# Gated attention and feed-forward on one core: value products in blocks of four key tiles from the first head, and three query products put off

## The chip, the core and the metric

One core of a Trainium2 chip runs the whole kernel. The metric is the device time of one execution in microseconds (us). The core's engines are TensorE (PE: matmuls, with weight loads as PEld), VectorE (DVE), ScalarE (ACT), GpSimdE (POOL) and SyncE (SP, which issues nearly all DMAs here). Each engine has its own instruction queue and works it off in order; engines wait for each other through semaphores. PE writes to PSUM, a small memory that ACT or DVE must empty before PE can use the same buffer again.

## What is computed

Input x has 2048 rows (tokens) of 512. There are 32 query heads of width 16, but one key and one value head; beside it a gated feed-forward of width 1792; a sigmoid gate per token mixes both.

```python
q = (x @ wq).reshape(B, S, 32, 16)          # 32 heads
k, v = x @ wk, x @ wv                       # one head
p = softmax(q @ k.T * 16 ** -0.5)           # per head, 2048 x 2048
a = (p @ v over all heads) @ wo
b = (silu(x @ w_gate) * (x @ w_up)) @ w_down
g = sigmoid((x * gate_w).sum(-1))
out = g * a + (1 - g) * b
```

All is float32. Projections are made of three products of rounded halves (high by high, high by low, low by high), so every operand is kept as a pair of tiles, `h` and `l`.

## The kernel before

**Numbering.** Token columns come in four chunks c of 512 (`CH`), query weights in four groups m of 128 columns (eight heads each), keys in 16 key tiles of 128. Query product (m, c) is the 128 x 512 piece of the queries for group m and chunk c; there are 16.

**Opening.** x is transposed chunk by chunk on PE, keys and values are projected, and the four query products of group 0 are made one after the other. Each is taken out of PSUM by `keep` (L208): a rounded copy `qh`, the rest `ql` by a subtraction, and a bound `qb` (|q| times the largest key, L218 or L221 and L222), whose maximum goes to `top` (L238). For group 0, `qh` and `qb` are made by ACT (L217, L218), for the others all by DVE. The pieces lie in tiles `hh` and `hl`, with seven buffers each; a buffer is free again when the DMA that stores it to `q_d` in DRAM (L232) has landed. SP issues the twelve stores of group 0 together (`run(STORES, NCH)`, L630), then the load of the last query weights (`load_wq(3)`, L631). Then `fill(GAP)` makes three more query products in full, (1,0), (1,1), (1,2). Heads after head 0 read their rows back from `q_d` (`load_head`, L640).

**Attention and feed-forward side by side.** From L771 on the order of instructions is written by hand. `score(u, j)` makes one half of a score tile (128 keys by 1024 queries, two matmuls on the two row halves of the array) into one of two PSUM buffers `pss`. `exps` takes the exponential on ACT into a tile `pt`. `mix(u)` makes the value products of tile u (L680) into `po`: they use the array in four column strips, unlike everything around them. In between, `feed` puts steps of a job list: each step is up to two matmuls on half the array's rows, the low rows of one job and the high rows of an earlier one (`Halves.step`, L385). Jobs are the query products, then the feed-forward's gate, up and down products. They use three PSUM buffers `pf`; when the high rows of a job are done, its end function empties the buffer.

**The order.** For heads 0 and 1 (32 tiles) a loop of `BEGIN = 16` rounds (L774 to L795) makes two tiles a round: four score halves, eight steps, then the value products of two tiles; all exponentials are taken by ACT straight from PSUM (form "A"). Then one longer block (`TURN`, L801) makes ten score halves, all of form "A", so that scores run two tiles ahead. From there on `block` (L711) makes four tiles a time by the string `STEPS`: eight score halves, 16 steps, then the value products of four tiles. In it three of the eight halves are of form "H": DVE copies the upper 512 columns out of PSUM (L664), ACT takes the exponential of the lower 512 from PSUM and of the upper 512 later from SBUF. Six `pt` buffers are needed for blocks; three come from pool `bp`, three from pool `bp2`, which is opened only when the last query product is made, in the memory of the query weights and of the x chunks 2 and 3 (`open_acc`, L248).

**Rows of x.** Chunks 0 and 1 stay in `xpool`; chunks 2 and 3 lie in `qpool` until the queries are done, are stored to `x_d`, and are read back (`load_x_again`) when the feed-forward has finished chunk 0 and chunk 1.

**End.** After the last block nine jobs are left; they run in full, and then the output projection (`finish`) closes the program.

## Time and profile before

| | |
|---|---|
| median of 3 runs (lowest, highest) | 1345.32 us (1343.87, 1346.47) |
| the profiled execution's own time | 1344.01 us |
| span of its instructions | 1341.9 us |
| mean granted TensorE clock | 0.999 |
| DVE, ACT, POOL busy, share of the span | 54%, 79%, 29% |
| DMA | 107.79 MB, 80 GB/s in the mean |

The span is 2.1 us shorter than the profiled execution's time; that is what lies around it. Rows of the timeline give start and duration in us, engine, line, operation, the tile written and the tiles read, and how many instructions the row merges; in brackets stands how long the engine was idle before, and what ended that. "SPq" is SP issuing a DMA.

### The profile page before, as it was taken

The numbers are of one execution on the slowest core, as the hardware profiler recorded it, in microseconds if no ns is written. First come the engines' busy times: TensorE is split into PE (matmuls) and PEld (weight loads), VectorE is DVE, ScalarE is ACT, GpSimd is POOL, SyncE is SP. The second block draws the span as 40 slices with busy tenths as digits, with TensorE's granted clock in tenths as the row PEclk, the third lists the DMA queues.
The fourth block names the chain that finished last, engine by engine and source line by source line (L and its number), as shares of the span: only waits on it lengthen the run. The fifth ranks groups of instructions, "written<-read, shape, count | busy, mean of one in ns | idle before, by whom it ended". The sixth has DMA issues, their size and how long they took to land. (4 is left out here: it accounts for less than half of the span.)

```text
span 1341.9 us, 26802 instructions
## 1 busy us (share of the span) xinstructions
PE 1328.0 (99%) x10743; PEld 770.4 (57%) x10743; DVE 722.4 (54%) x1221; ACT 1061.6 (79%) x1463; POOL 391.0 (29%) x408
## 2 busy tenths in 40 slices
PE   9999999999999999999999999999999999999997
PEld 7655555555555555555555555555555555555576
DVE  5554565555455555555464555455454565465432
ACT  4578888888888888888888888888888888888400
POOL 6140321152042151152131241142131241333343
PEclk9999999999999999999999999999999999999999
DMA  8455221131122221141131221231121221222154
GB/s 277 142 173 190 65 60 38 35 107 44 44 86 77 78 80 38 35 107 44 52 122 39 82 79 39 57 83 45 52 61 30 81 79 39 74 68 60 44 161 143
DMA packets 101489, 107.79 MB, mean 80 GB/s; under 512 B 9968, under 2 KB 69616, under 8 KB 99696
## 3 DMA queue, kind: packets, MB, share of 16 engines
q1 hardware_dynamic: 99632, 105.81, 27.5%
q8 instruction: 88, 1.44, 0.5%
q10 hardware_dynamic: 1728, 0.20, 0.1%
q14 instruction: 41, 0.34, 0.1%
HBM read 76.09 MB, written 29.36 MB: 79 GB/s over the span
## 5 line engine op out<-in xcount | busy, mean ns | idle before, releaser
L668 ACT ACTIVATE pt<-pss 128x1024 f32<-128x1024 f32 (+1 forms) x1024 | 842.0, 876 | 177.3 <-PE pss L660 146.3
L664 DVE COPY pt<-pss 128x512 f32<-128x512 f32 x354 | 244.8, 692 | 415.6 <-PE pss L660 380.6
L680 PE MATMUL po<-pt,vaug 128*32 128x512 f32 x4096 | 467.6, 595 | 0.0
L660 PE MATMUL pss<-qs,ks 64*128 64x512 f32 x2048 | 403.1, 417 | 1.1 <-ACT pt L668 1.1
L660 PEld LDWEIGHTS pss<-qs,ks 64*128 64x128 f32 x2048 | 193.7, 184 | 218.4 <-ACT pt L668 183.6
L680 PEld LDWEIGHTS po<-pt,vaug 128*32 128x32 f32 x4096 | 119.2, 109 | 260.2 <-issue 255.2
L668 ACT ACTIVATE pt<-pt 128x512 f32<-128x512 f32 x354 | 195.7, 620 | 0.0
L176 PE MATMUL pf<-xh,wgl 64*128 64x512 f32 (+1 forms) x440 | 162.0, 392 | 0.0
L176 PE MATMUL pf<-xh,wgh 64*128 64x512 f32 (+1 forms) x440 | 160.5, 391 | 0.5 <-DVE acc L331 0.2
L176 PE MATMUL pf<-xl,wgh 64*128 64x512 f32 (+1 forms) x440 | 160.2, 390 | 0.0
L176 PE MATMUL pf<-xh,wuh 64*128 64x512 f32 (+1 forms) x440 | 158.4, 391 | 0.7 <-DVE sign L403 0.3
L176 PE MATMUL pf<-xl,wuh 64*128 64x512 f32 (+1 forms) x440 | 158.2, 390 | 0.0
L176 PE MATMUL pf<-xh,wul 64*128 64x512 f32 (+1 forms) x440 | 157.3, 391 | 0.0
L106 POOL CAST wgh<-wraw 128x512 fp32r<-128x512 f32 x56 | 36.1, 644 | 402.6 <-PE pf L176 311.8
L176 PE MATMUL pf<-wdh,hh 64*128 64x512 f32 (+1 forms) x427 | 143.4, 391 | 1.7 <-DVE hh L106 1.7
L176 PE MATMUL pf<-wdh,hl 64*128 64x512 f32 (+1 forms) x427 | 144.1, 390 | 0.0
L176 PE MATMUL pf<-wdl,hh 64*128 64x512 f32 (+1 forms) x427 | 143.4, 390 | 0.0
L689 DVE RECIPROCAL rsb<-rsb 128x128 f32<-128x128 f32 x128 | 117.1, 935 | 10.1 <-issue 8.2
L106 POOL CAST wuh<-wraw 128x512 fp32r<-128x512 f32 x56 | 35.1, 626 | 298.2 <-PE pf L176 245.3
L176 PEld LDWEIGHTS pf<-xh,wgh 64*128 64x128 f32 (+1 forms) x440 | 78.5, 185 | 9.8 <-issue 2.5
L176 PEld LDWEIGHTS pf<-xh,wuh 64*128 64x128 f32 (+1 forms) x440 | 77.3, 185 | 9.3 <-issue 3.7
L176 PEld LDWEIGHTS pf<-xl,wgh 64*128 64x128 f32 (+1 forms) x440 | 78.5, 185 | 6.0
(157 smaller groups left out, 1547.6 us busy)
## 6 DMA issues: line engine op xcount, KB each, us to landing
wraw<-in_B_w_gate_dram SPq DMA_DIRECT2D x56, 256.0 KB
wraw<-in_B_w_up_dram SPq DMA_DIRECT2D x56, 256.0 KB
wraw<-in_B_w_down_dram SPq DMA_DIRECT2D x56, 256.0 KB
qs<-q_d SPq DMA_DIRECT2D x62, 192.0 KB
q_d<-hl SPq DMA_DIRECT2D x18, 256.0 KB
q_d<-hh SPq DMA_DIRECT2D x18, 256.0 KB
o_d<-osb SPq DMA_DIRECT2D x128, 32.0 KB
a_d<-acc SPq DMA_DIRECT2D x4, 1024.0 KB
```

The source lines that it names most:

```text
L106: eng_hi.tensor_copy(hi, src)
L176: ins = nc.tensor.matmul(self.ps, a, b, start=(i == 0 and not half), stop=(last and half != 0))
L660: nc.tensor.matmul(ps[:, b * CH:(b + 1) * CH], ks[rows, kt * P:(kt + 1) * P], QS[h][rows, j, :], start=True, stop=True)
L664: other = nc.vector.tensor_copy(pt[:, CH:], ps[:, CH:]) if half else None
L668: ins = nc.scalar.activation(pt[:, w], ps[:, w], AF.Exp, scale=SCALE)
L680: nc.tensor.matmul(po[c * 2 * DH:(c + 1) * 2 * DH, :], vaug[:, kt, :], pt[:, c * CH:(c + 1) * CH], start=(kt == 0), stop=(kt == NT - 1))
L689: nc.vector.reciprocal(rsb[:, w], rsb[:, w])
```

## The change

- **Blocks from the first tile.** The loop of two-tile rounds and the long `TURN` block are gone. A short opening `OPEN` makes four score halves (form "A") and eight steps; then `block` is called for all 128 groups of four tiles.
- **Six `pt` buffers in one pool.** For this the memory of `qpool` must be free when attention begins. The query weights and the value tile `vz` are laid into the three buffers of the later feed-forward sums (`HOME`), and x chunks 2 and 3 are given up at the same point.
- **Which query products run when.** `fill(GAP)` now makes (1,2), (1,3) and (2,3) in full, since they need chunks 2 and 3. In the blocks run the six products of groups 1 to 3 on chunks 0 and 1. Three, (2,2), (3,2), (3,3), wait until chunks 2 and 3 have been read back for the feed-forward, and are put among its jobs (`places`).
- **Who empties them.** The three early ones are now emptied by ACT (copy and bound) and DVE (subtraction), as group 0's are. For the six and the three late ones DVE copies and subtracts at once, and the three instructions of the bound go to the list `DEFER`, which a block works off at its end. The late ones use a weight buffer `wraw` for `ql` and an output buffer `osb` for the bound.
- **One load earlier.** `load_wq(3)` is issued ahead of the twelve stores of group 0.

```diff
-PTB = 3
+PTB = 6
-BEGIN = 16
+EARLY_Q = ((1, 2), (1, 3), (2, 3))
+LATE = ((2, 2), (3, 2), (3, 3))
-TURN = "SS" + "SFF" * 8
+OPEN = "SFSFFFSFFFSF"
...
+    accp = tc.alloc_tile_pool(name="accp", bufs=3, side="right")
+    HOME = [accp.tile([P, TC, D], F32, name="acc") for _ in range(3)]
...
         def keep(ps):
...
+            late = (m, c) in LATE
+            behind = late or m and c in ORDER[:2]
+            if late:
+                qh = hp.tile([P, CH], F32R, name="qh", bufs=1)
+                ql = wp.tile([P, CH], F32, name="wraw", bufs=WRB).bitcast(F32R)
+            else:
+                qh = wp.tile([P, CH], F32R, name="hh", bufs=7)
+                ql = wp.tile([P, CH], F32R, name="hl", bufs=7)
-            if m:
+            if behind:
...
                 nc.vector.tensor_copy(qh, ps)
             else:
                 qb = wp.tile([P, CH], F32R, name="hl" if c % 2 else "hh", bufs=7).bitcast(F32)
                 nc.scalar.activation(qh, ps, AF.Copy)
                 nc.scalar.activation(qb.bitcast(F32R), ps, AF.Abs, scale=kmax)
             nc.vector.tensor_tensor(ql, ps, qh.bitcast(F32), ALU.subtract)
...
+            if behind:
+                store([0, 1])
+                DEFER.extend([((m, c), 0.5, scale), ((m, c), 0.7, bound), ((m, c), 0.7, most)])
...
-        jobs = [query(m, c) for m in range(1, KD) for c in range(NCH)]
...
+        return [query(m, c) for m, c in EARLY_Q] + [query(m, c) for c in ORDER[:2] for m in range(1, KD)]
...
+    last = [query(m, c) for m, c in LATE]
+    places = {(1, 0): last[:1], (1, 1): last[1:2], (2, 0): last[2:]}
...
+                    if j == 4:
+                        yield from places.get((m, GROUPS.index(fs)), ())
...
+            load_wq(3)
             run(STORES, NCH)
-            load_wq(3)
             fill(GAP)
...
-            for j in range(2):
-                exps(*score(0, j))
-            for n in range(BEGIN):
...
-                settle()
-                mix(u)
-                mix(u + 1)
...
-            for k in range(2 * BEGIN // BLOCK, NB):
+            tiles = [(u, j) for u in range(2) for j in range(2)]
+            for what in OPEN:
+                if what == "S":
+                    exps(*score(*tiles.pop(0)))
+                else:
+                    feed(1)
+            for k in range(NB):
                 u = BLOCK * k
-                if k == 2 * BEGIN // BLOCK:
...
-                    block(k, u + 1, u + 6, TURN, "A" * 2 * n, [f"{i}d" for i in range(2 * n)])
```

**Where instructions stand: ACT at the beginning of attention.** Before, the last bound of group 0 is followed at once by the exponentials. Names carry the program's buffer numbers; in brackets stand the semaphores that the instruction waits for (PE, DVE, Activation, Pool; `DMAHW` are landings of DMAs).

```order
L217 ACTIVATE hh_525<-pf_512 128x512 [waits PE_49]
L218 ACTIVATE hl_527<-pf_512,kmax_83 128x512
L668 ACTIVATE pt_696<-pss_697 128x1024 [waits DMAHW3_49,DMAHW2_49,DMAHW4_49,DMAHW1_49,DMAHW5_49,DMAHW0_49,DMAHW6_49,PE_49,DMAHW7_49,Activation_49,Pool_49]
L668 ACTIVATE pt_696<-pss_701 128x1024 [waits PE_49]
L668 ACTIVATE pt_712<-pss_713 128x1024 [waits PE_49]
L668 ACTIVATE pt_712<-pss_719 128x1024 [waits PE_49]
```

Of the change, from the copy of query product (1,2) on (`pf_550`; `pf_573` is (1,3), `pf_596` is (2,3)):

```order
L229 ACTIVATE hh_563<-pf_550 128x512 [waits PE_49]
L690 ACTIVATE pt_690<-pss_691 128x1024 [waits DMAHW3_49,DMAHW4_49,DMAHW2_49,DMAHW5_49,DMAHW1_49,DMAHW6_49,DMAHW0_49,DMAHW7_49,PE_49,Activation_49]
L230 ACTIVATE hh_565<-pf_550,kmax_83 128x512 [waits DMAHW6_49,DMAHW4_49,Activation_49]
L229 ACTIVATE hh_586<-pf_573 128x512 [waits DMAHW7_49,Activation_49]
L230 ACTIVATE hl_588<-pf_573,kmax_83 128x512 [waits DMAHW5_49]
L690 ACTIVATE pt_690<-pss_697 128x1024 [waits PE_49]
L229 ACTIVATE hh_609<-pf_596 128x512 [waits DMAHW1_49,DMAHW2_49,DMAHW0_49,DVE_49]
L230 ACTIVATE hl_611<-pf_596,kmax_83 128x512 [waits DMAHW2_49,DMAHW3_49,DVE_49,Activation_49]
L690 ACTIVATE pt_704<-pss_705 128x1024 [waits PE_49]
```

Five instructions that empty query products have moved onto ACT between the first, second and third exponential, and each of them waits for landings of DMAs.

**PE at the same place.** Before, two score halves (`pss`) are followed by steps of query product (1,3) (`pf_705`):

```order
L660 MATMUL pss_697<-qs_257,ks_78 128x512 x2
L660 MATMUL pss_701<-qs_257,ks_78 128x512 x2
L176 MATMUL pf_705<-xh3_325,wq1h_411 128x512
L176 MATMUL pf_705<-xl3_326,wq1h_411 128x512
L176 MATMUL pf_705<-xh3_325,wq1l_412 128x512
```

Of the change, where `pf_695` is query product (1,0):

```order
L179 MATMUL pf_596<-xh3_328,acc_95 128x512
L682 MATMUL pss_691<-qs_261,ks_78 128x512 x2
L179 MATMUL pf_695<-xh_170,acc_94 128x512
L682 MATMUL pss_697<-qs_261,ks_78 128x512 x2
L179 MATMUL pf_695<-xl_171,acc_94 128x512
```

A step of a fourth product now stands behind the first score half; it needs one of the three `pf` buffers, which the three early products hold.

**SP after the last rows of head 0.** Before:

```order
L228 DMA qs_257<-hl_527 16x512
L232 DMA q_d_69<-hl_439 8x16x512
L232 DMA q_d_69<-hh_438 8x16x512
L232 DMA q_d_69<-hh_440 8x16x512
L232 DMA q_d_69<-hl_478 8x16x512
L232 DMA q_d_69<-hh_477 8x16x512
L232 DMA q_d_69<-hl_479 8x16x512
```

Of the change:

```order
L237 DMA qs_261<-hl_525 16x512
L201 DMA wraw_534<-in_A_wq_dram 128x4x128
L242 DMA q_d_69<-hl_437 8x16x512
L242 DMA q_d_69<-hh_436 8x16x512
L242 DMA q_d_69<-hh_438 8x16x512
L242 DMA q_d_69<-hl_476 8x16x512
L242 DMA q_d_69<-hh_475 8x16x512
L242 DMA q_d_69<-hl_477 8x16x512
```

The load of the last query weights has moved ahead of the stores, whose order is the same.

More of the change, by code (lines that the diff above doesn't have):

```diff
@@ L195, in load_wq @@
     def load_wq(m):
-        WQ[m] = load_split(wq_v[:, :, m * P:(m + 1) * P], f"wq{m}", 1, qpool)
+        home = HOME[2 if m > 1 else 1]
+        raw = wp.tile([P, KD, P], F32, name="wraw", bufs=WRB)
+        nc.sync.dma_start(raw, wq_v[:, :, m * P:(m + 1) * P])
+        WQ[m] = [home[:, m % 2 * 2 + j, :].rearrange("p (k n) -> p k n", k=KD).bitcast(F32R) for j in range(2)]
+        split(*WQ[m], raw, nc.gpsimd, nc.gpsimd)
     def query(m, c):
@@ L325, in add @@
             if c not in ACC:
-                ACC[c] = PAIR[0].tile([P, TC, D], F32, name="acc")
+                assert len(ACC) < 2 or not any(query in JOBS for query in last)
+                ACC[c] = accp.tile([P, TC, D], F32, name="acc")
             acc = ACC[c]
```

78 lines of the change are left out of this document (28 added, 50 removed).

## The prediction

> **What bounds the kernel now.** I read the page's busy times first, then the busy times of three stretches (columns: PE, weight loads, DVE, ACT, POOL, granted clock, DMA share, GB/s).
>
> ```profile
> PE 1328.0 (99%) x10743; PEld 770.4 (57%) x10743; DVE 722.4 (54%) x1221; ACT 1061.6 (79%) x1463; POOL 391.0 (29%) x408
> 48.00:128.40 80.40, 80.40 (x646) 43.20 (x646) 42.75 (x76) 63.12 (x67) 19.91 (x20) 1.00 0.57 189
> 128.40:141.00 12.60, 11.65 (x89) 5.16 (x85) 5.70 (x10) 9.29 (x11) 2.92 (x3) 1.00 0.59 159
> 141.00:216.30 75.30, 75.30 (x641) 41.96 (x641) 43.30 (x75) 66.20 (x93) 20.51 (x21) 1.00 0.22 57
> ```
>
> PE is the bound: busy all through the rounds of two tiles (first stretch) and the blocks (third), short of work only in the long block between them (second). But "busy" hides switching between forms of the array. That shows in the distance from one group of value products to the next, in PE's timeline:
>
> ```profile
> 53.37 1.92 PE L680 MATMUL po<-pt,vaug 128*32 128x512 f32 x16
> 126.50 1.92 PE L680 MATMUL po<-pt,vaug 128*32 128x512 f32 x16
> 137.35 3.64 PE L680 MATMUL po<-pt,vaug 128*32 128x512 f32 x32
> 212.63 3.64 PE L680 MATMUL po<-pt,vaug 128*32 128x512 f32 x32
> 114.31 0.39 PE L176 MATMUL pf<-xl,wgh 64*128 64x512 f32 x1
> 114.54 0.39 PE L176 MATMUL pf<-xh,wgl 64*128 64x512 f32 x1
> ```
>
> The first two rows are the first and the last of 16 rounds: 73.13 us for 15 distances, 4.875 each. The next two are nine groups apart by count, eight distances: 75.28, 9.41 each. One step (or score half) takes 0.23, as the last two rows start.
>
> **Term 1, fewer switches: -2.7.** Four tiles cost 2 x 4.875 = 9.75 in rounds and 9.41 in a block, with the same eight score halves and 16 steps. 32 tiles are eight fours: 8 x 0.34 = 2.7. The program has as many steps as before and leaves nine jobs to the end as before, so no work moves to the tail.
>
> **Term 2, the long block goes: -2.7.** It lasts 126.50 to 137.35, 10.85. PE's own need would be a block's 9.41, less 1.72 (the value products ahead of it take 1.92, not 3.64), plus two more score halves, 0.46: 8.15. The other 2.7 are waits for ACT:
>
> ```profile
> 128.96 9.27 ACT L668 ACTIVATE pt<-pss 128x1024 f32<-128x1024 f32 x10 [0.54 <-PE pss L660]
> 130.03 0.50 PE L660 MATMUL pss<-qs,ks 64*128 64x512 f32 x2 [0.95 <-ACT pt L668]
> ```
>
> ACT takes ten exponentials without a pause, and each later score half waits for one. The change builds the lead of two tiles at the beginning of attention instead, so what is late next stands there.
>
> **Term 3, the new beginning: +7.1.** The order of the three engines there is shown above. These rows say what was there before:
>
> ```profile
> 39.88 0.60 ACT L217 ACTIVATE hh<-pf 128x512 fp32r<-128x512 f32 x1 [1.54 <-PE pf L176]
> 40.37 0.68 ACT L218 ACTIVATE hl<-pf,kmax 128x512 fp32r<-128x512 f32 x1
> 41.09 0.69 DVE L219 TENSOR_TENSOR hl<-pf,hh 128x512 fp32r<-128x512 f32 x1 [1.44 <-ACT hl L218]
> 43.63 0.77 SPq L232 DMA_DIRECT2D q_d<-hl  x1
> 44.45 1.29 SPq L232 DMA_DIRECT2D q_d<-hh  x2
> 47.93 0.73 PE L660 MATMUL pss<-qs,ks 64*128 64x512 f32 x4
> 48.62 3.77 ACT L668 ACTIVATE pt<-pss 128x1024 f32<-128x1024 f32 x4 [7.57 <-issue]
> 49.42 0.69 DVE L214 CAST hh<-pf 128x512 fp32r<-128x512 f32 x1 [3.57 <-DMA q_d<-hh]
> 51.09 2.54 SPq L232 DMA_DIRECT2D q_d<-hh  x2
> ```
>
> The row at 49.42 decides. DVE stood 3.57 us, because the eighth tile `hh` takes the buffer of the first, and that is free only when the second store of group 0 has landed. DVE's wait cost nothing: PE had other buffers. In the change ACT makes that tile, the bound of (1,2), and ACT's exponentials are queued behind it. Later stores follow at 1.27 (51.09: two in 2.54). From the order in which buffers are taken, the bound of (1,2) needs the second store, the copy of (1,3) the third, the copy of (2,3) the fifth and its bound the sixth: 49.4, 50.7, 53.2, 54.5 on the clock of before.
>
> The load of the last query weights now goes ahead of the stores. SP took this long for such a load:
>
> ```profile
> 4.61 0.47 SPq L137 DMA_DIRECT2D wraw<-in_A_wq_dram  x1
> 24.30 2.64 SPq L137 DMA_DIRECT2D wraw<-in_A_wq_dram  x2
> ```
>
> That is 0.47, or 1.3 each of two. I take the middle, 0.9: the queue is idle here, but the load's 256 KB pass ahead of the stores. Then the four are 50.3, 51.6, 54.1, 55.4. Step by step:
> - The first score half and its exponential stay at 47.93 and 48.6 to 49.6.
> - Bound of (1,2): 50.3 to 51.0 (0.68). DVE's subtraction comes after the bound, as at 41.09, and ends at 51.7. Only then is a `pf` buffer free, and the step behind PE's first score half starts at 51.8. PE stands from 48.2 to 51.8; the second score half waits behind that step.
> - Copy and bound of (1,3), 1.2 for both by the rows at 39.88 and 40.37: to 52.8. Second exponential (3.77 / 4 = 0.94): to 53.8.
> - Copy of (2,3) at 54.1, bound 55.4 to 56.1; third and fourth exponential to 58.1. The fifth and sixth score halves wait for these two PSUM buffers.
> - From 58.2 the sixth half, 16 steps and six halves: 23 x 0.23 = 5.3; with 0.2 for the switch the first value products start at 63.7.
>
> By then PE has done 12 score halves and 24 steps. Before, at 53.37, it had done six and 16; 14 more at 0.23 end at 56.6. So the beginning loses 63.7 - 56.6 = 7.1. Ends: 0.4 less or more for the load; 4.5 in all if no landing is waited for (rival 1).
>
> **Term 4, emptying query products beside blocks: +0.7.** Copy and subtraction hold a `pf` buffer for two DVE instructions, a gate product for one. These rows are the query product (3,3) of before, the first and the last of its five instructions:
>
> ```profile
> 120.31 0.69 DVE L214 CAST hh<-pf 128x512 fp32r<-128x512 f32 x1 [3.65 <-PE pf L176]
> 122.89 0.69 DVE L238 TENSOR_REDUCE top<-ht 128x1 f32<-128x512 f32 x1
> ```
>
> Nine products run this way. In the order of the change the next step that needs the buffer stands at least eight steps or halves (1.8 us) later, at one place, after (3,2), seven (1.6); with a half copy ahead on DVE it is 0.7 + 1.4 = 2.1. I count 0.5 there and 0.2 for the rest. Below, the end is 0: in the rounds nine such products cost PE no wait. Above, it is 9 x 0.69 = 6.2, if none is hidden. I stay by the lower end, since DVE is busy 43.30 of 75.30 us in blocks. The three instructions of the bound, put off to the end of a block, lie beside value products; without that room they would hold the half copies and so the scores.
>
> **At nothing.** Feed-forward weights are needed earlier, since only six query products are ahead of them:
>
> ```profile
> 79.02 0.61 POOL L106 CAST wgh<-wraw 128x512 fp32r<-128x512 f32 x1 [12.65 <-DMA wraw<-in_B_w_gate_dram]
> 110.36 0.39 PE L176 MATMUL pf<-xh,wgh 64*128 64x512 f32 x1
> ```
>
> The split that begins at 79.02 is over by 81; the first gate step, before at 110.36, comes at about 63.7 + 3 x 9.41 + 4 = 96, still 15 later. SP's stores and loads are otherwise as many as before; the row reads of head 1 stay behind 21 stores. The late products write `ql` into a weight buffer, whose load was issued about a block (9.4) before; if it were not split by then, DVE would stand with its half copies queued behind.
>
> **Sum.** -2.7 - 2.7 + 7.1 + 0.7 = **+2.4**. Against the profiled execution that is 1344.01 + 2.4 = 1346.4; the median shown is 1.3 above that execution, so I forecast **1347.7**, 0.18% above. (About 0.2%, 2.7 us, is what a measurement of this kernel can tell from no change.)
>
> **A rule against the change.** First the rows: busy times before and after the last matmul, which ends at 1336.2, with the granted clock third from the end.
>
> ```profile
> 1336.40:1339.40 3.00, 0.00 (x0) 0.00 (x0) 0.72 (x2) 0.00 (x0) 0.00 (x0) 1.00 0.32 98
> 1339.50:1341.90 2.40, 0.00 (x0) 0.00 (x0) 0.00 (x0) 0.00 (x0) 0.00 (x0) 0.50 0.02 7
> ```
>
> PE's clock halves after some 3.2 us without work. Nowhere else between its first and last matmul does PE stand so long. In the new beginning it stands 3.6. [...]
>
> **Rivals.**
> - *Rival 1, landings do not bind* (the queue is quicker than I read it). Then only ACT's order counts: bound (1,2) 49.5 to 50.2, step at 51.0, (1,3) to 51.4, second exponential to 52.4, (2,3) to 53.6, fourth exponential to 55.5, value products at 61.1: 4.5 in place of 7.1, sum -0.2, **1345.1**. Against it stand the 3.57 us at 49.42.
> - *Rival 2, the clock drops*, and the kernel ends slower. [...] It decides as soon as it adds 0.3 to the forecast. For it: the idle time is longer than the one that sufficed at the end. Against: steps from 51.8 on may count as work.
> - *Rival 3, the change does what it says* and ACT is held by nothing but exponentials. For the last score half ten must be done: seven at 0.94 and three halves at 0.60, 8.4 from 48.6 on, 57.0; value products at 57.7, a loss of 1.1: sum -3.6, **1341.7**. Against it is ACT's order.
> - *Rival 4, DVE gets in the way*: term 4 at its upper end, 6.2: sum +7.9, **1353.2**. For it: half copies and landings share one queue. Against: DVE's idle 43%.
>
> The 0.60 is this row's mean:
>
> ```profile
> L668 ACT ACTIVATE pt<-pss 128x512 f32<-128x512 f32 x354 | 211.0, 596 | 11.6
> ```
>
> **How the numbers follow.** Forecast 0.50 (own range 1346.3 to 1349), rival 1 0.13, rival 2 0.18, rival 3 0.12, rival 4 0.07. The range 1344.3 to 1350.5 leaves out rivals 3 and 4. Faster by over 0.2% (below 1342.6): rival 3, 0.12. Slower (above 1348.0): rivals 2 and 4, and 0.20 of the forecast's 0.50: 0.45. The rest, 0.43, is within 0.2%.
>
> **What would show it.** In the changed profile: value products 9.41 apart from the first on (term 1), no stretch with ten exponentials in a row (term 2), PE idle some 3.6 us near 48 with DVE's subtraction as what ended it, ACT idle before its bound with a store of `hh` as what ended it, and the first value products at 63.7 (term 3). The ninth group should start at 139.0 against 137.35. First value products near 58 would prove me wrong in term 3; distances well above 9.41 among the first nine groups, in term 4.

## The result and the profile after

The changed kernel takes 1356.45 us (median of 6 runs, 1355.70 to 1357.57), the kernel before 1345.49 in the runs beside it: ratio 1.0085, 95% interval 1.0075 to 1.0095. It is slower by 11 us, where 2.4 were forecast. The profiled execution took 1356.18 us, of which the span is 1354.3; before it was 1344.01 and 1341.9. The 12.4 us between the spans divide so (each row from PE's timeline; the first ends where the ninth group of value products of a block's form starts):

| stretch of the span | before | after | difference | forecast |
|---|---|---|---|---|
| up to the ninth group | 137.35 | 144.86 | +7.5 | +1.7 |
| from there to the last group | 1121.8 | 1124.2 | +2.4 | +0.7 |
| from the last group to the end | 82.8 | 85.2 | +2.5 | 0 |

The busy times on the profile's page of the changed kernel say little by themselves. PE does as many matmuls as before and is busy 4.5 us longer:

```profile
PE 1332.5 (98%) x10743; PEld 777.1 (57%) x10743; DVE 736.0 (54%) x1239; ACT 1069.8 (79%) x1496; POOL 391.2 (29%) x408
```

**The beginning.** PE's timeline of the changed kernel (start, length, idle time before it and what ended it): the first score half, the two places where PE stood, and the first, the ninth and the last group of value products.

```profile
48.14 0.50 PE L682 MATMUL pss<-qs,ks 64*128 64x512 f32 x2
51.83 0.49 PE L179 MATMUL pf<-xh,acc 64*128 64x512 f32 x1 [3.20 <-DVE hl L231]
...
57.64 1.71 PE L682 MATMUL pss<-qs,ks 64*128 64x512 f32 x4 [1.53 <-ACT pt L690]
...
67.79 3.64 PE L702 MATMUL po<-pt,vaug 128*32 128x512 f32 x32
144.86 3.64 PE L702 MATMUL po<-pt,vaug 128*32 128x512 f32 x32
1269.06 3.64 PE L702 MATMUL po<-pt,vaug 128*32 128x512 f32 x32
```

Up to the step at 51.83 all is as the prediction drew it. ACT's and DVE's timelines of the same time show the cause, too: ACT's bounds (L230) wait until stores have landed, as the copies (L229) between them do, and exponentials (L690) are queued behind them.

```profile
48.75 1.02 ACT L690 ACTIVATE pt<-pss 128x1024 f32<-128x1024 f32 x1 [5.35 <-DMA q_d<-hl]
50.37 0.69 ACT L230 ACTIVATE hh<-pf,kmax 128x512 fp32r<-128x512 f32 x1 [0.59 <-DMA q_d<-hh]
...
55.98 0.69 ACT L230 ACTIVATE hl<-pf,kmax 128x512 fp32r<-128x512 f32 x1 [0.68 <-DMA q_d<-hl]
56.57 3.42 ACT L690 ACTIVATE pt<-pss 128x1024 f32<-128x1024 f32 x4
```

```profile
51.09 0.69 DVE L231 TENSOR_TENSOR hl<-pf,hh 128x512 fp32r<-128x512 f32 x1 [8.51 <-ACT hh L230]
```

What was not drawn so is the clock. Busy times of three stretches, with the granted clock third from the end:

```profile
47.80:53.00 5.20, 2.00 (x11) 1.08 (x10) 1.28 (x2) 2.67 (x4) 1.08 (x1) 1.00 0.52 189
53.00:66.70 13.70, 12.05 (x43) 8.67 (x42) 4.70 (x8) 8.87 (x12) 0.00 (x0) 0.50 0.53 203
66.70:77.40 10.70, 10.70 (x92) 5.80 (x94) 4.40 (x9) 8.70 (x14) 0.00 (x0) 1.00 0.69 224
```

It is 0.50 for 13.7 us, from about 1.2 us behind the end of PE's standing to just ahead of the first value products, which start at 67.79 and not at 63.7. The sixth score half starts at 58.55, close to the forecast (58.2); from there to the value products it is 9.24 us, where the prediction has 5.5. Behind them the next eight distances sum to 77.07 (144.86 - 67.79), where eight times 9.41 are 75.28: 1.8 more, all of it in the first five distances, whose blocks carry the query products.

**The middle.** Three distances are 10.56, 10.54 and 10.53, where the kernel before has 9.79, 9.41 and 9.42: 3.0 us together. The others differ by at most 0.4 us from those of the kernel before, and are 0.6 shorter in sum. PE's and DVE's timelines at the three places:

```profile
276.87 0.47 PE L179 MATMUL pf<-xh,wgh 64*128 64x512 f32 x1 [0.87 <-DVE sign L425]
...
456.56 0.50 PE L179 MATMUL pf<-xh,wuh 64*128 64x512 f32 x2 [0.84 <-DVE wraw L231]
...
571.02 0.49 PE L179 MATMUL pf<-xh,wuh 64*128 64x512 f32 x1 [0.83 <-DVE sign L425]
```

```profile
274.71 0.69 DVE L686 COPY pt<-pss 128x512 f32<-128x512 f32 x1 [0.75 <-ACT pt L690]
275.32 0.68 DVE L300 SCALAR_TENSOR_TENSOR ht<-ht,hs 128x512 f32<-128x512 f32 x1
276.03 0.69 DVE L310 TENSOR_TENSOR ht<-ht,pf 128x512 f32<-128x512 f32 x1
...
455.81 0.69 DVE L231 TENSOR_TENSOR wraw<-pf,qh 128x512 fp32r<-128x512 f32 x1 [1.08 <-POOL wdl L110]
...
568.90 0.69 DVE L686 COPY pt<-pss 128x512 f32<-128x512 f32 x1 [0.75 <-ACT pt L690]
569.51 0.68 DVE L226 CAST qh<-pf 128x512 fp32r<-128x512 f32 x1
570.28 0.69 DVE L231 TENSOR_TENSOR wraw<-pf,qh 128x512 fp32r<-128x512 f32 x1
```

At 456 and 571 a late query product is emptied; the third, at 769, costs nothing. At 276 it is an `up` product whose silu instruction (L300) was not done yet, so it too takes two DVE instructions. In the first and the last case these stand behind a copy of a score half.

**The tail.** Near 1290 PE stands at two places, where it stood at one before (1.66 us at 1281), and the clock is halved for 3.4 of the ten us around them:

```profile
1289.31 0.50 PE L179 MATMUL pf<-wdl,hh 128*128 128x512 f32 x1 [0.48 <-POOL wdl L110]
1292.15 0.76 PE L179 MATMUL pf<-wdh,hh 128*128 128x512 f32 x1 [2.11 <-DVE hh L109]
```

```profile
1289.00:1299.00 10.00, 7.58 (x25) 5.83 (x26) 5.06 (x6) 0.00 (x0) 5.87 (x7) 0.83 0.32 96
```

POOL's first cast of an output weight shows where this begins. The first row is of the kernel before, the second of the changed one:

```profile
1260.37 0.61 POOL L106 CAST wo0h<-wraw 128x512 fp32r<-128x512 f32 x1 [27.71 <-PE po L680]
```

```profile
1272.85 0.61 POOL L109 CAST wo0h<-wraw 128x512 fp32r<-128x512 f32 x1 [30.34 <-PE po L702]
```

Both wait for value products. Before, the cast starts 1.2 us behind the start of the last group (1259.14); now 3.8 behind it (1269.06), when all of that group is done. The down-projection weights come through POOL behind it.

### The profile page after: what moved, and what is told of

Same layout as the page of the kernel before. It is cut to its first block, busy times and chain, and to the rows that moved or that the text cites. A ratio compares the mean times of both kernels' runs of the same rounds, so it can differ in the third digit from the quotient of the medians.

```text
span 1354.3 us, 26884 instructions
## 1 busy us (share of the span) xinstructions
PE 1332.5 (98%) x10743; PEld 777.1 (57%) x10743; DVE 736.0 (54%) x1239; ACT 1069.8 (79%) x1496; POOL 391.2 (29%) x408
## 5 line engine op out<-in xcount | busy, mean ns | idle before, releaser
L690 ACT ACTIVATE pt<-pss 128x1024 f32<-128x1024 f32 (+1 forms) x1024 | 833.3, 864 | 174.4 <-PE pss L682 144.0
L686 DVE COPY pt<-pss 128x512 f32<-128x512 f32 x381 | 263.4, 692 | 430.9 <-PE pss L682 392.0
L682 PEld LDWEIGHTS pss<-qs,ks 64*128 64x128 f32 x2048 | 196.9, 184 | 214.0 <-ACT pt L690 174.4
L690 ACT ACTIVATE pt<-pt 128x512 f32<-128x512 f32 x381 | 210.7, 620 | 0.1
L179 PE MATMUL pf<-xh,wuh 64*128 64x512 f32 (+1 forms) x440 | 155.5, 392 | 2.2 <-DVE sign L425 1.0
L179 PE MATMUL pf<-xl,wuh 64*128 64x512 f32 (+1 forms) x440 | 155.0, 390 | 0.0
```

The source lines that it names most:

```text
L179: ins = nc.tensor.matmul(self.ps, a, b, start=(i == 0 and not half), stop=(last and half != 0))
L682: nc.tensor.matmul(ps[:, b * CH:(b + 1) * CH], ks[rows, kt * P:(kt + 1) * P], QS[h][rows, j, :], start=True, stop=True)
L686: other = nc.vector.tensor_copy(pt[:, CH:], ps[:, CH:]) if half else None
L690: ins = nc.scalar.activation(pt[:, w], ps[:, w], AF.Exp, scale=SCALE)
```

## The experiments

All of them start from the changed kernel. Times are medians, the ratio is against the kernel before on the same chip; the other columns are of the profiled execution, in us.

| run | median | ratio, 95% interval | first group | ninth group | ninth to last | last to end |
|---|---|---|---|---|---|---|
| changed kernel | 1356.45 | 1.0085 (1.0075, 1.0095) | 67.79 | 144.86 | 1124.2 | 85.2 |
| early_dve | 1351.23 | 1.0041 (1.0027, 1.0056) | 59.92 | 139.20 | 1124.3 | 85.1 |
| filler | 1356.37 | 1.0079 (1.0062, 1.0096) | 69.49 | 146.26 | 1127.5 | 85.0 |
| filler2 | 1355.38 | 1.0070 (1.0053, 1.0088) | 65.94 | 143.02 | 1125.5 | 84.6 |
| wo_pad_j3 | 1356.16 | 1.0089 (1.0072, 1.0105) | 67.26 | 144.03 | 1125.1 | 83.8 |
| split | 1354.13 | 1.0055 (1.0039, 1.0072) | 68.84 | 146.09 | 1124.5 | 81.8 |
| ql_hs_lean | 1356.29 | 1.0080 (1.0063, 1.0097) | 68.92 | 145.56 | 1123.9 | 85.1 |
| fix3 | 1347.09 | 1.0007 (0.9997, 1.0017) | 60.18 | 138.35 | 1124.3 | 82.7 |
| fix5 | 1358.48 | 1.0084 (1.0067, 1.0101) | 60.80 | 146.52 | 1127.1 | 83.6 |
| fix6 | 1345.12 | 1.0002 (0.9993, 1.0011) | 61.41 | 139.63 | 1121.7 | 82.7 |
| fix7 | 1345.21 | 1.0001 (0.9992, 1.0010) | 59.84 | 137.97 | 1122.1 | 84.3 |
| fix8 | 1344.19 | 0.9983 (0.9973, 0.9993) | 62.01 | 139.39 | 1122.1 | 83.1 |

### Who empties the early query products (early_dve)

```diff
-            behind = late or m and c in ORDER[:2]
+            behind = late or bool(m)
```

> The changed kernel, with its three early query products emptied by DVE (cast, subtraction, scale, bound, maximum) instead of by ACT and DVE; nothing else is changed. Theory A (the emptying by ACT, whose bound needs a buffer that a store still holds, keeps a product buffer from the first step and the idle PE then loses its clock): PE does not stand near 48 (3.20 us in the changed kernel), the granted clock stays at 1.0 between 53 and 67 (0.50 there now), the first value products start at 59 to 61 instead of 67.79 and the ninth group at 136 to 138 instead of 144.86; median 1347 to 1349. Theory B (landings of the stores bind whoever empties, since the cast needs such a buffer too): PE still stands 2 us or more near 48, first value products at 65 or later, median 1353 or more.

The first value products start at 59.92, the largest gap of PE from 47 to 60 is 0.44, and the clock stays:

```profile
53.00:67.00 14.00, 13.11 (x99) 7.87 (x101) 7.83 (x15) 10.89 (x16) 0.00 (x0) 1.00 0.53 203
```

This is theory A, and the largest single part of the loss: 7.9 us at the first group, 5.2 in the medians. Its ranges for the ninth group and the median are missed all the same (139.20, 1351.23). What is lost between is in blocks 6 and 7 (counted from 0): the ninth group comes 79.28 behind the first and not 77.07. There PE stands 1.68 us, because DVE waits for the landing of a store of `hs`:

```profile
114.01 0.48 DVE L245 TENSOR_SCALAR hs<-hh,kmax 128x512 f32<-128x512 f32 x1 [4.06 <-DMA q_d<-hs]
```

SP's queue has three stores of 256 KB for each of nine products, 1.0 to 1.4 us apart there. That the faster start meets a backlog of transfers, which the slow start had hidden, is a reading that no run shows: in fix3 the start is as early and this wait is gone.

### Is it the standing that costs the clock? (filler, filler2)

60 small products into an unused tile stand behind the first score half; the second run, whose edit is shown in part, has 54 more ahead of the third score half.

```diff
+        def keep_on(n):
+            for i in range(n):
+                nc.tensor.matmul(spare[:, :P], cold[:, :P], cold[:, :P], start=True, stop=True)
...
+                    if n == 6:
+                        keep_on(54)
                     exps(*score(*tiles.pop(0)))
+                    if n == 0:
+                        keep_on(60)
```

> The changed kernel, with 60 small products into an unused tile that PE runs behind the first score half, where it stands from 48.6 to 51.8 (the start's own products of this kind come 0.056 us apart: 3.4 us). They compute nothing that is used. Theory A (the standing itself costs the clock of the next 13.7 us): the waits of the first step stay, the granted clock between 53 and 67 is 1.0 instead of 0.50, the first value products start at 63.7 instead of 67.79, as the sum on record had them, and the median falls by 4 us, to 1352 to 1353. Theory B (the clock falls because PE is only half busy between 53 and 67, waiting for ACT's and DVE's emptying): the clock there stays at 0.5 or falls a little later, first value products at 66.5 or later, median 1355 to 1357.

Theory B's numbers came out (the clock fell later, first value products at 69.49, median 1356.37), but the trace points to another standing as the reason. PE's timeline of filler, and busy times with the clock of two stretches:

```profile
49.20 3.52 PE L802 MATMUL po<-ident 128*128 128x128 bf16 x60
52.80 0.49 PE L180 MATMUL pf<-xh,acc 64*128 64x512 f32 x1
...
58.46 0.80 PE L683 MATMUL pss<-qs,ks 64*128 64x512 f32 x2 [3.23 <-ACT pt L691]
```

```profile
56.00:60.00 4.00, 1.54 (x5) 0.78 (x5) 1.28 (x2) 3.32 (x5) 0.00 (x0) 0.75 0.53 204
60.00:64.00 4.00, 3.80 (x14) 2.83 (x13) 0.95 (x3) 2.04 (x4) 0.00 (x0) 0.50 0.52 202
```

The steps from 52.80 on ran at full clock, so PE was through with them sooner and stood 3.23 us at the next place, for the exponentials behind ACT's emptying (1.53 in the changed kernel). The edit did one thing more than it was meant to: in both runs with small products ACT takes the second exponential only behind the last early bound (57.40 in filler), and not between the bounds (53.11 in the changed kernel). Then the clock fell after all. Another gap, of 2.05 at 459, cost it once more from 460.8 to 464.2, which is a part of this run's 1127.5 in the table.

> The changed kernel with two stretches of small products into an unused tile, 60 behind the first score half as in the run with one stretch, and 54 more (3.2 us) ahead of the third score half, where PE stood 3.23 us in that run (from 55.2 to 58.46, for the exponentials that stand on ACT behind the emptying of the query products) and where the clock then fell to 0.5. They compute nothing that is used. Theory A (a standing of about 3 us at either place costs the clock, and with both filled it stays): the granted clock is 1.0 from 8 to 1285, the first value products start at 64 to 65 instead of 67.79 (69.49 with one stretch), the ninth group at 140.5 to 142 instead of 144.86, the median is 1352 to 1353.5. Theory B (the clock falls for something else than the standing): 0.5 for 10 us or more between 50 and 70, first value products at 67 or later, median 1355.5 to 1357.

With both places filled the clock did not fall there, as theory A has it (busy times of filler2):

```profile
47.00:53.00 6.00, 6.00 (x73) 5.08 (x71) 0.90 (x2) 1.75 (x3) 1.90 (x2) 1.00 0.56 188
53.00:67.00 14.00, 13.41 (x122) 9.67 (x123) 5.15 (x10) 11.15 (x17) 0.00 (x0) 1.00 0.53 203
```

The price is read from the sixth score half on, behind which PE waits no more in either run (first row the changed kernel; the others filler2, PE's and then ACT's timeline):

```profile
58.55 0.79 PE L682 MATMUL pss<-qs,ks 64*128 64x512 f32 x2
```

```profile
60.38 0.50 PE L682 MATMUL pss<-qs,ks 64*128 64x512 f32 x2 [0.41 <-ACT pt L690]
65.94 3.64 PE L702 MATMUL po<-pt,vaug 128*32 128x512 f32 x32
57.49 4.25 ACT L690 ACTIVATE pt<-pss 128x1024 f32<-128x1024 f32 x5
```

To the first value products it is 5.56 us here and 9.24 in the changed kernel: the half clock costs 3.7 us. From the first score half on (49.20 in this execution, 48.14 in the changed kernel's) it is 16.74 instead of 19.65, only 2.9 less, since in filler2 ACT takes three exponentials and not two between the last bound and that half. Theory A's other numbers are missed: the clock also fell once at the beginning (0.86 in the mean from 8 to 20), the first and the ninth group are 0.9 and 1.0 above their ranges, and the median is 1355.38. It is only 1.1 us lower, where 3 to 4.5 were expected; in the profiled execution the start is 1.06 later and the gap at 276 is 1.53 instead of 0.87, which takes back 1.7.

### Where the output weights lie (wo_pad_j3, split)

The first run puts 16 KB of unused memory ahead of the output weights and, for the next section, the late products at another place in their groups.

```diff
+        tp.tile([P, 2 * S], F32, name="pad", bufs=1)
         for k in range(KD):
             load_wo(k, tp)
...
-                    if j == 4:
+                    if j == 3:
```

> The changed kernel with two edits that touch different places. First, an unused tile of 16 KB per partition ahead of the output weights in the last pool, so that these lie where the tiles of exponentials of earlier key tiles lay and not where the last ones did. Theory A (POOL's first cast of an output weight waits, 30.34 us, for the very last value product, because it overwrites that tile, and this delays the last down-projection weights): the cast starts 2 us or more before the end of the last value products (3.8 us behind their start now, 1.2 in the kernel before), PE's gaps of 0.48 and 2.11 near 1290 shrink to 1.7 together or less and the clock does not fall there; 2 to 3 us. Theory B (another wait takes its place, the loads' own): gaps as they are. Second, the three late query products stand behind the fourth product of their group instead of the fifth, which ends them at steps 19, 15 and 3 of blocks 39, 51 and 73 instead of at steps 8, 13 and 15 of blocks 41, 53 and 74. Theory A (the gaps of 0.84 and 0.83 at 456.56 and 571.02 hang on the step at which two DVE instructions empty such a product): both go, 2 us; the 0.87 at 276.87, of an up product, stays. Theory B (a late product costs this wherever it stands): two or three gaps near 0.8 at the new places. Median 1351 to 1352.5 with A in both, 1356 with B in both.

The pad did nothing: the cast still starts when the last group is done (1272.91, the last group from 1269.11 on). That fits a wait for the last reader of the whole pool whose memory the output weights take, 3.8 us behind the group's start as in the changed kernel, and not of one tile. PE's gaps in the tail stay at 0.46 and 2.00; only the clock did not fall there this time (0.39 to 0.50 us a matmul behind the second gap, 0.63 to 0.76 in the changed kernel), and the tail is 83.8. So the second run gives the tiles two pools of three, as before the change:

```diff
-                PT[u] = bp.tile([P, S], F32, name="pt", bufs=PTB)
+                first = u % PTB in (2, 3, 4)
+                PT[u] = (bp if first else bp2).tile([P, S], F32, name="pt", bufs=PTB // 2)
```

> The changed kernel, with the six tiles of exponentials in two pools of three, as in the kernel before: the pool whose memory the output weights take over at the end then holds key tile 124 last, and no longer 127. Theory A (that POOL's first cast of an output weight waits for the last reader of that pool sets the tail): the cast starts 1.2 to 1.5 us behind the start of the last value products instead of 3.8, PE's gaps 0.48 and 2.11 near 1290 become none and 1.4 to 1.8, the granted clock does not fall there (0.83 over ten us there now), the stretch from the last value products to the end shrinks from 85.2 to 82.8 to 83.4 us, and the median is 1353.5 to 1354.5. Theory B (the tail is set by the loads of the weights and of the attention rows): it stays at 84.8 or more, median 1356 to 1357.

POOL's timeline, with the last group at 1270.59, and then PE's only gap near 1290:

```profile
1271.81 0.61 POOL L109 CAST wo0h<-wraw 128x512 fp32r<-128x512 f32 x1 [27.71 <-PE po L703]
```

```profile
1292.36 0.47 PE L179 MATMUL pf<-wdh,hh 128*128 128x512 f32 x1 [1.58 <-DVE hh L109]
```

The cast starts 1.2 us behind the group's start, the gap at POOL's weights is gone, and the tail is 81.8 us instead of 85.2. The median is 2.3 lower. The tail's loss is shown to come from the merging of the two pools: 1 to 2 us by the waits (83.8 in wo_pad_j3, where they stand and the clock held; 81.8 here, and 82.7 to 83.1 in fix3, fix6 and fix8 below), the rest by the half clock behind them.

### What a late product costs, and what fills the first blocks (ql_hs_lean, second half of wo_pad_j3)

```diff
-                ql = wp.tile([P, CH], F32, name="wraw", bufs=WRB).bitcast(F32R)
+                ql = wp.tile([P, CH], F32, name="ht" if (m + c) % 2 else "hs", bufs=2).bitcast(F32R)
...
-                store([0, 1])
-                DEFER.extend([((m, c), 0.5, scale), ((m, c), 0.7, bound), ((m, c), 0.7, most)])
+                store([0, 1, 2] if lean else [0, 1])
+                if not lean:
+                    DEFER.extend([((m, c), 0.5, scale), ((m, c), 0.7, bound), ((m, c), 0.7, most)])
```

> The changed kernel with two edits. First, the low rows of the late query products go to a buffer of the feed-forward (ht or hs) and not to the weights' raw buffer. Theory A (at 455.81 DVE's subtraction waits 1.08 us for POOL, which still reads that buffer): the wait and PE's 0.84 at 456.56 go; the 0.83 at 571.02 stays, where DVE did not wait for POOL; 1.1 us. Theory B (the wait is the queue of instructions ahead on DVE): both stay. Second, the six query products in the blocks leave out their scale, bound and maximum on DVE and store their high rows in the place of the bound, so the output is not the reference's. Theory A (these instructions fill DVE in blocks 1 to 5 and cost the 1.8 us by which these five groups stand over 9.41 each): the distances of the second to sixth groups fall to 9.4 to 9.5 each, ninth group 1.3 to 1.8 us earlier than 144.86. Theory B (the cast and the subtraction alone, which hold a product buffer, cost it): less than 0.6 us. Median 1353.5 to 1354.5 with A in both.

The gap at 456 is gone and the one at 571 stays (0.89): in the first, DVE waited for POOL's use of the buffer. The second half fell to theory B: without scale, bound and maximum the first eight distances sum to 76.64, 0.4 less than 77.07. In filler and wo_pad_j3, whose blocks keep these instructions, they sum to 76.8. So the rest of the 1.8 us, some 1.4, stays when these instructions are gone. The trace of ql_hs_lean shows how most of it arises (PE's timeline, then DVE's):

```profile
85.67 0.50 PE L686 MATMUL pss<-qs,ks 64*128 64x512 f32 x2 [0.19 <-DVE sign L429]
```

```profile
83.53 0.68 DVE L228 CAST hh<-pf 128x512 fp32r<-128x512 f32 x1
84.24 0.69 DVE L233 TENSOR_TENSOR hl<-pf,hh 128x512 fp32r<-128x512 f32 x1
84.85 0.68 DVE L690 COPY pt<-pss 128x512 f32<-128x512 f32 x1
```

The copy of a score half stands on DVE behind the cast and the subtraction, and PE's next score half comes only when it is done. What is late is thus the score's `pss` buffer, not only a `pf` buffer. The second and the fifth distance hold such a wait and are 9.94, with and without the put-off instructions: 1.1 us of the 1.4. (The tick on `sign`, to which the profile puts the wait down, is DVE's next instruction behind the copy.) The first and the fourth distance are 0.15 longer without a wait that the trace shows, and their cause stays open. No run took the cast and the subtraction away. The median, 1356.29, did not fall as theory A in both has it; the mean granted clock of its profiled execution, 0.991, is the lowest of all runs in the table.

Moved by one product (`j == 3`), the late products caused no gap in block 39, but 0.41 and 0.37 at 569 and 598, and one distance 0.57 longer at 751. The gap at 276, which the edit leaves alone, is 1.40 here; in the five other runs up to here it is 1.22 to 1.53, and the 0.87 of the changed kernel's profile is the least of all. So the stretch from the ninth group to the last did not shrink (1125.1). Neither theory had that: the place matters, and why the new places cost what they do was not tried.

### The corrections together (fix3, fix5, fix6, fix7, fix8)

fix3 is early_dve with the buffer of ql_hs_lean and the pools of split.

> Three edits together: the early query products emptied by DVE alone, the low rows of the late ones in a feed-forward buffer, the tiles of exponentials in two pools. If the effects add: first value products at 59.9, PE's waits of 1.68 and 0.46 in blocks 6 and 7 stay as in the run with the first edit alone (DVE waits 4.06 us there for the landing of a store of hs), no gap over 0.3 in block 41, tail 82.8 to 83.4 us, median 1348 to 1349 against 1351.23 with the first edit alone. If the tail or the late products are hidden behind something else: 1350.5 or more.

It came out 0.9 us under the lower end for effects that add, and is the same as the kernel before (interval 0.9997 to 1.0017). The wait of 1.68 us in block 6 was gone too, though nothing was done to it; the 0.46 in block 7 became 0.62. The clock was at half once in the opening, for 3.4 us from 55.0.

fix5 is fix3 with a longer opening and an output buffer for the last bound.

```diff
-OPEN = "SFSFFFSFFFSF"
+OPEN = "SFSFFFFSFFFFSFFF"
...
-                qb = hp.tile([P, CH], F32, name="osb") if late else wp.tile(...
+                qb = hp.tile([P, CH], F32, name="osb") if late or (m, c) == (3, 1) else wp.tile(...
```

> The run before with two more edits. First, the bound of the last query product in the blocks goes to an output buffer (osb) and not to hs, so that DVE has no store of hs to wait for: PE's wait of 1.68 us in block 6 goes. Second, the opening takes 12 feed-forward steps instead of 8, which moves every later product against the blocks' steps. Theory A (a product that two DVE instructions empty at once, held back to step 13 of a block, costs 0.8 to 1.4 us because DVE copies score halves ahead of it; at 8 steps that is an up product in block 22 and a late query product in block 53): those two gaps go, one of 0.8 to 1.4 us appears in block 58, where an up product ends at step 13 with both instructions, and the three late products, now at steps 4, 7 and 8 of blocks 41, 53 and 74, cost nothing. Median 1345 to 1346.5. Theory B (late products cost about 1 us each wherever they stand): gaps of 0.8 or more in blocks 41, 53 or 74; median 1347 or more.

It missed by 12 us, and for a reason that neither theory named. With four more steps in the opening, the first `gate` product of the third feed-forward slice is reached before its weights (first row), which POOL begins to split at 122.1, as it does in fix3:

```profile
122.74 0.80 PE L179 MATMUL pf<-xh,wgh 64*128 64x512 f32 x2 [5.54 <-POOL wgh L109]
...
570.34 0.47 PE L179 MATMUL pf<-xh,wuh 64*128 64x512 f32 x1 [0.59 <-DVE ht L231]
...
620.75 0.50 PE L179 MATMUL pf<-wdh,hh 64*128 64x512 f32 x1 [1.46 <-DVE sign L425]
```

The matmuls behind the 5.54 us ran at half clock: a row of two takes 0.63 at 123.33, where it takes 0.40 at 123.02 in fix3. On the theory of step 13 the run was half right. The gap of block 22 was gone and the one foretold for block 58 came, at 620.75; but the late product at step 7 of block 53 still cost 0.59.

fix6 is fix3 with two other edits. It leaves the opening as it was and takes away the two instructions at step 13 in another way:

```diff
-BUDGET = 3.8
+BUDGET = 4.0
...
-                    if j == 4:
+                    if j == {(1, 0): 3, (1, 1): 2, (2, 0): 4}.get((m, GROUPS.index(fs))):
```

> The run with three edits (DVE empties the early query products, a feed-forward buffer for the late ones' low rows, two pools of exponentials) with two more. First, the budget of put-off DVE work of a block is 4.0 instead of 3.8, so that the silu instruction of block 22's up product is done at the end of block 21 and one DVE instruction empties that product at step 13 instead of two. Second, the late products stand behind the fourth, third and fifth product of their groups, which ends them at steps 19, 3 and 15 of blocks 39, 48 and 74; none is at 13. Theory A (two DVE instructions at step 13 are what costs): no gap over 0.3 in block 22 (1.66 now) and in block 53 (0.87 now), none over 0.3 in blocks 39, 48 and 74; the stretch from the ninth group to the last falls from 1124.3 to 1121.5 to 1122.3 us, as in the kernel before (1121.8); median 2 to 2.8 us under 1347.09. Theory B (put-off or moved work turns up as waits elsewhere): 1123.5 or more, median 1346 or more.

The stretch from the ninth group to the last is as in the kernel before, with no gap over 0.3:

```profile
139.63:1261.32 1121.69, 1120.10 (x9446) 627.70 (x9444) 623.89 (x1059) 970.77 (x1359) 300.21 (x307) 1.00 0.23 63
```

So the middle's 2.4 us are the three collisions on DVE. The median is 1.97 lower than fix3's, but the kernel before is 1.56 lower on this chip, too: by the ratios 0.7 us are gained. The price stands in block 3, where the larger budget lets one more maximum go ahead of the copies of score halves, and where two bounds took 1.66 and 1.67 us (0.98 and 0.69 in fix3):

```profile
88.08 0.50 PE L683 MATMUL pss<-qs,ks 64*128 64x512 f32 x2 [1.25 <-DVE sign L425]
```

fix7 is fix6 with the output buffer of fix5 and a later load:

```diff
-                if k % (NT // BLOCK) == 0 and 0 < h < H - 1:
+                if k % (NT // BLOCK) == 1 and 0 < h < H - 1:
```

> The same with two more edits for blocks 6 and 7: the rows of a head after the next are loaded one block later (four transfers, 3.5 us of SP's queue at 110 to 114, ahead of the gate weights that POOL waits for until 122.0), and the bound of the last query product in the blocks goes to an output buffer instead of hs. If the backlog of transfers sets the start of these blocks: the wait of 0.62 us for POOL's weights near 124 goes, the ninth group starts 0.8 to 1.3 us earlier against the first value products than in the run with three edits (78.2 us behind them), and the median is 0.8 to 1.3 us under the run beside it. If the weights come late for another reason: same as that run within 0.5 us.

The wait in block 7 is gone, but the ninth group comes 78.13 behind the first (78.23 in fix6, which has no such wait either): no gain. The second theory holds for the median.

fix8 is fix7 with the larger budget from block 8 on only:

```diff
-            left = BUDGET
+            left = BUDGET if k < 2 * NT // BLOCK else BUDGET + 0.2
```

> The run with seven edits, with the larger budget of put-off DVE work (4.0) only from block 8 on and 3.8 before it. In blocks 0 to 7 the larger budget lets a maximum of a query product go ahead of block 3's copies of score halves, and PE stands 1.22 us there. If that is the whole cost of the larger budget: no gap over 0.4 in block 3, the ninth group 76.8 to 77.2 us behind the first value products instead of 78.12, the blocks behind it 1121.7 to 1122.3, and the median 0.8 to 1.3 us under 1345.21, at 1343.9 to 1344.4, which is within 0.2% of the kernel before. If the put-off maximum only moves the wait to blocks 4 to 7: same as 1345.21 within 0.5 us.

The gap in block 3 is 0.51, the ninth group 77.38 behind the first: part of the wait went. The rest is there without that maximum, which was thus not the whole cost. Its median, 1344.19, is 0.17% under the kernel before as it ran on that chip (1346.93); on the chips of the other runs the kernel before took 1344.55 to 1346.11. This version is as fast as the kernel before, or faster by up to 0.3%.

## Why the prediction failed

The time (1356.45) lies above the range. The order of events was right; three sizes were not, and one part of the change was not priced.

- **Terms 1 and 2** hold as far as they go: no stretch with ten exponentials in a row is left, and from the ninth group on the blocks are 9.4 apart as before. In the first eight blocks, though, where term 1 had its gain, the distance is 9.63 in the mean: of the 2.7 us, 0.9 are left.
- **Term 3** failed in its last step, "23 x 0.23 = 5.3". The step at 51.8, the bound's wait for the second store and the fourth exponential's end near 58 came as drawn (51.83, behind a standing of 3.20 and not 3.6; 50.37; the first two of the four in the row at 56.57). But those 23 steps and halves ran at half clock: 9.24 us from the sixth score half to the value products, where the prediction has 5.5. Of the 4.1 us at the first group that is 3.7; the sixth half itself starts 0.35 late. The prediction had the falling clock as rival 2 and weighed it at 0.18; the clock stayed at 0.50 until 66.7, which is nearly all of the 23. filler2, at full clock, takes 5.56 us for the same stretch: the prediction's sum was right for that clock. The last two stretches of 3.41 us at half clock show that 3.4 us of full work (PE's busy time comes second in a row) did not bring the clock back at once; it was 1.00 again after the second:

```profile
59.86:63.28 3.42, 3.42 (x12) 2.72 (x13) 1.00 (x3) 1.20 (x3) 0.00 (x0) 0.50 0.53 205
63.28:66.69 3.41, 3.41 (x18) 2.62 (x18) 0.69 (x1) 2.04 (x3) 0.00 (x0) 0.50 0.52 202
```

  Behind the last matmul of the kernel before, 3.2 us passed until the clock was halved; the 3.20 us here were enough, too.
- **Rival 1** (landings do not bind) is refuted: ACT's bounds at 50.37 and 55.98 waited for landings. early_dve takes the landings and the emptying off ACT together, and starts the value products at 59.92; the rival, which left the emptying on ACT, had 61.1.
- **Term 4** had two errors. In all, 0.7 was counted and 4.2 measured. For the products in the first blocks 0.2 was counted and 1.8 measured, 1.1 of it since copies of score halves stand behind the cast and the subtraction. The argument "DVE is busy 43.30 of 75.30 us" was an average; what counts is what stands ahead on DVE at the step where the buffer is needed. For the late products it had one place, (3,2), with 0.5; two places, (2,2) at 456 and (3,2) at 571, cost 1.1 each, the first of them by the wait for POOL's split of the weight buffer, which the prediction named ("DVE would stand with its half copies queued behind") and costed at nothing. The third collision, of an `up` product at 276, comes from the shifted phase between products and blocks and was not foreseen.
- **"No work moves to the tail"** was true of the work and wrong of the time: 2.5 us came from one pool of six tiles in the place of two of three. With one pool POOL's first cast of an output weight waited for the last value product (3.8 us behind the start of its group, 1.2 with the two pools of split). split takes it back. A part of the 2.5 us is the half clock in the tail.
- **Rival 3** (the change does what it says) and **rival 4** (DVE in the way, +7.9) each have a part of the truth. Rival 3 is refuted for the opening, where ACT's order and the landings did bind. The blocks make 1.8 + 2.4 = 4.2 us of the 12.4, most of it by collisions on DVE, where rival 4 had up to 6.2. With the corrections of fix8 the change is worth 0 to 0.3%; rival 3's 3.6 us would be 0.27%.

## What to carry to other kernels

In these runs a wait of PE of 3.20 us, put where PE had none, was followed by 13.7 us of half clock, and one of 3.23 by 10.2. Where a change puts such a wait, count on that, and price it by all the work in such a stretch, not by a few instructions; and look for the next wait in the row, since filling one only uncovered the other. On DVE, whose copy of a score half stood behind a cast and a subtraction (83.53 to 84.85 in ql_hs_lean), an average idle share did not say that an instruction is hidden: find the step at which its result is needed and list what stands ahead of it there. And when pools are merged or split, ask who reads them last, and what is loaded into that memory next.

## What the runs showed of the hardware

- **The half clock came in pieces.** In the changed kernel it lasted 13.65 us from 53.03 on and 3.41 from 1292.07 on, and in filler 10.2 from 58.0 on: 4, 1 and 3 times 3.41. It was 3.4 us in filler at 460.8, in fix3 at 55.0, in fix6 near 57 and in the tail of fix7. The stretches at full clock between and behind them in the changed kernel, 1225.39 and 58.03 us, are 359 and 17 times 3.413. So in this trace the five changes of the clock lie on one grid of 3.413 us. Laid on it from 5.25 on, the clock fell behind the three intervals at full clock in which PE was idle for 2.21, 2.51 and 3.41 us, and behind none of the other 387, with 1.66 at most. In the kernel before, on the same grid laid back from its one change at 1339.42, it fell behind 3.21 us and behind none of the other 390, with 1.65 at most. Of the 3.20 us of the changed kernel, 2.2 lay in one interval:

```profile
49.62:53.03 3.41, 1.20 (x7) 0.93 (x8) 1.28 (x2) 1.83 (x4) 0.00 (x0) 1.00 0.52 197
```

  Elsewhere less standing went with one piece. In fix6 the largest gap of PE between 47 and 60 was 0.52, in fix7 0.43, with 1.58 and 1.27 us idle in sum from 47 to 60.5; the clock fell in the first (first row fix6, second fix7):

```profile
57.00:60.50 3.50, 3.36 (x16) 2.92 (x18) 1.87 (x3) 1.95 (x4) 0.00 (x0) 0.51 0.52 200
```

```profile
57.00:60.50 3.50, 3.42 (x30) 2.51 (x34) 1.88 (x4) 2.83 (x6) 0.00 (x0) 1.00 0.52 200
```

  In the tail the clock fell behind a gap of 1.60 us in fix7 (0.63 us a matmul), and not behind gaps of 1.58 to 1.66 in the kernel before, split, fix3 and fix6 (0.39 to 0.50 us a matmul). A gap of 2.00 came with the fall in filler2 and without it in wo_pad_j3. What decides in these cases is not shown.
- **DVE beside POOL.** In fix6 the bound of a query product (L248) took 1.66 us while POOL split weights (a subtraction from 81.89 to 83.24). The second bound there (84.95, 1.67 us) and two of the changed kernel (88.10 and 98.05, 1.66 each) started during such a subtraction, too; all four ended 0.55 or 0.56 us behind its end. The six bounds of the changed kernel that met no work of POOL took 0.69. Why the four took longer is not shown:

```profile
82.14 1.66 DVE L248 SCALAR_TENSOR_TENSOR hs<-hs 128x512 fp32r<-128x512 f32 x1
```

- **Stores of 256 KB** into the query scratch went out about 1.25 us apart in early_dve between 50 and 65, where many follow each other (2.40 for two at 52.61, 1.31 at 55.06; all DMAs together moved 203 GB/s from 53 to 67). The 21 stores of group 0 and the early products kept SP's queue busy there from 45 to 70.6.
